# Three passes instead of four for the last 64 queries, keys turned over in place, and the first MoE's relu earlier in the order

## The chip, the core and the metric

The kernel runs on one core of a Trainium2 chip. The core has a matrix engine (TensorE; PE in the profile, with its weight loads shown apart as PEld), a vector engine (VectorE, DVE), a scalar engine (ScalarE, ACT), a general one (GpSimd, POOL) and a queue engine (SyncE, SP) that issues nearly all DMAs here. Each engine works through its own list of instructions in a fixed order, and semaphores hold an instruction until what it needs is there. The metric is the device time of one launch in microseconds (us). Before the change it is 1017.72 us, the median of three runs that lie between 1014.41 and 1018.50.

## What is computed

Three steps follow each other, all in float32 (the weights of the two MoEs come as float64):

```
# attention: 4 batches, 8 heads, 576 positions, 64 wide
scores = (q @ k.T) / 8 + cum[query] - cum[key]      # cum: running sum of log f
scores = where(key > query, -1e9, scores)
attn   = softmax(scores) ; x = attn @ v             # -> 2304 tokens x 512
# first MoE: 512 -> 2048 -> 512
h = x @ w_in ; g = max(0.01 * h, h) ; y = g @ w_out
# second MoE: 512 -> 1536 -> 512
out = ((y @ w_a) * (y @ w_b)) @ w_o
```

## The kernel before

**Parts of a number.** A float32 value is kept as a rounded part (type F32R, called high) and a rest (low); a product needs three matmuls: high by high, high by low, low by high. The first MoE's inputs are the pairs `xh`, `xl`; its relu gives `gh` and `gl`.

**Attention.** A batch is worked off as two blocks `(b, r)`: r=0 has queries 0 to 255, r=1 queries 256 to 575 (320 queries against all 576 keys). Within a block the heads come in pairs; `hp` is the pair, `j` is 0 or 1 for its first or second head. In names such as `s4_2_1_3_0` the numbers are batch, block, head and piece. Batch 0 uses plain float32; batches 1 to 3 do as follows (`att_scores`, L322 to L450):

- A head's queries are loaded twice, one copy in each half of the 128 partitions, and turned over 32 by 32 on DVE into `tq` (L326). `qhh` is their high part (ACT, L337), `qll` the rest (DVE, L338).
- The keys of both heads of a pair are loaded into `xk`, one head in each half of the partitions, and turned over by DVE into another tile, `tk` (L350). There are two `xk` buffers, taken in turn by the pairs, and one `tk`.
- For each head, `ks` (three buffers) has the keys' high part in one half of the partitions (ACT, L356) and their low part in the other (DVE, L357). One matmul of `qhh` with `ks` so gives high queries by both parts of the keys, and a second one with `qll` the low queries by both parts.
- Queries 256 to 511 go 128 at a time through `score`, two passes a tile. The last 64 queries of the two heads of a pair share one tile `s4` of 128 rows, worked off with the second head (j=1): `qhh` and `qll` of either head have 64 blank columns beside their last 64 queries, so that head h-1 adds to the first 64 rows alone and head h to the other 64. The 576 keys are cut in two pieces of 288 columns. That is four passes of 128 by 288 a piece (L432 to L440): `qhh` and `qll` of head h-1 with its `ks`, and `qhh` and `qll` of head h with its own.

DVE then adds scores and decay and takes the row's extreme (L402, L444); ACT does the exponential (L373) and the normalisation (L411, L540); PE turns the probabilities over (`pp`) and multiplies by the values (`av`), two heads at once; ACT and DVE bring the result into `xh` and `xl`.

**First MoE.** Tokens go in 9 groups of 256, the inner width in 8 units per group: `work(i, pr)` calls `l1` (24 matmuls of 256 columns into `h`, then the relu) and, one unit late, `l2` (12 matmuls of 512 columns into `y`). `h` has one buffer. The relu is two instructions on ACT, `gh` (rounded) and `hs` (plain), L881 and L882, and one on DVE, `gl`, L884.

**Order.** Apart from the first block, whose order is a table written out by hand, a scheduler lays the instructions of each engine in a row before the run. It goes by the order in which the program issues them; `tc.high_priority(offset=n)` lets an instruction count as issued n instructions earlier. Block (b, r) is issued in the middle of a group's units, so attention's instructions fill in among the MoE's on all engines. SP's loads are in that order as well, and a load that waits for its buffer holds up all loads behind it. The second MoE follows after all attention; its layers use seven products in place of eight on quarters of the matrices.

Of the kernel before, what the change touches and what calls it, by code (L numbers as in the profile page):

```python
# [8 lines left out]
F32 = mybir.dt.float32  # L9
F32R = mybir.dt.float32r  # L10
# [4 lines left out]
ALU = mybir.AluOpType  # L15
# [3 lines left out]
P = 128  # L19
# [7 lines left out]
def kernel(  # L27
# [14 lines left out]
    B, H, S, D = q.shape  # L42
# [9 lines left out]
    SCALE = 1.0 / float(D) ** 0.5  # L52
# [67 lines left out]
    pe_att, act_att, dve_att, pool_att = (Ahead(e) for e in (nc.tensor, nc.scalar, nc.vector, nc.gpsimd))  # L120
# [12 lines left out]
    def f32(ap):  # L133
        return ap.bitcast(F32)
# [128 lines left out]
    def att_scores(b, r, h, st):  # L263
# [3 lines left out]
        hp, j = h // 2, h % 2  # L267
# [46 lines left out]
        else:  # L314
# [15 lines left out]
            lasts[h] = qhh, qll  # L330
            z0 = 64 if r == 1 and j == 1 else 0
            if r == 1:
                blank = slice(320, 384) if j == 0 else slice(0, 64)
                for part in (qhh, qll):
                    pool_att.memset(f32(part[:, blank]), 0.0)
            zq = slice(z0, z0 + nq)
            act_att.mul(qhh[:, zq], tq[:, :nq], -SCALE)  # L337
            dve_att.scalar_tensor_tensor(  # L338
                out=qll[:, zq], in0=tq[:, :nq], scalar=-SCALE, in1=f32(qhh[:, zq]), op0=ALU.mult, op1=ALU.subtract
            )  # L340
            if j == 0:
                xk = ap_.tile([P, 18, 32], F32, tag=("xk", "xk2")[hp % 2], name=f"xk_{nm}")
                for u in range(2):
                    for e in range(2):
                        nc.sync.dma_start(
                            xk[u * 64 + e * 32 : u * 64 + e * 32 + 32, :nkc, :],
                            k[b, h + u, 0:nk, e * 32 : e * 32 + 32].rearrange("(c i) d -> i c d", i=32),
                        )
                tk = ap_.tile([P, S], F32, tag="tk", name=f"tk_{nm}")
                dve_att.transpose(out=tk[:, :nk], in_=xk[:, :nkc, :].rearrange("p c d -> p (c d)"))  # L350
                qks[pair] = tk

            ks = lastk[h] = ap_.tile([P, S], F32R, tag="ks", bufs=3, name=f"ks_{nm}")
            o = 64 - a
# [2 lines left out]
            dve_att.tensor_tensor(  # L357
                out=ks[o : o + 64, :nk], in0=tk[a : a + 64, :nk], in1=f32(ks[a : a + 64, :nk]), op=ALU.subtract
            )

            def score(o, c0, cols_):
                pe_att.matmul(o, qhh[:, c0 : c0 + P], ks[:, cols_], start=True, stop=False)
# [50 lines left out]
        if r == 1:  # L413
            if j == 0:
                p4s[b, hp] = ap_.tile([P, S], F32, tag="p4", name=f"p4_{nm}")
            p4 = p4s[b, hp]
            st4 = ap_.tile([P, 1], F32, tag="st4", bufs=2, name=f"st4_{nm}")
            made = pool_att.tensor_scalar(
                p4[a : a + 64, :], cumb[a : a + 64, :], 1.0, ncum_t4[a : a + 64, b * HP + hp : b * HP + hp + 1],
                op0=ALU.mult, op1=ALU.add,  # L420
            )
            if (b, h) == (0, 0):
                tc.add_manual_dep(made.ins, quiet[0].ins.name, SYNC, reason="second block's decay behind the fourth pair")
            pool_att.affine_select(
                out=p4[a : a + 64, 512:S], in_=p4[a : a + 64, 512:S], pattern=[[-1, 64]], base=0,
                channel_multiplier=1, compare_op=ALU.is_ge, fill=MASKED,
            )
            for c in range(2):
                if b and j == 0:
                    break  # L430
                sl = slice(c * 288, c * 288 + 288)
                sp = score_bank(b, pair, j, (4, c), f"s4_{nm}_{c}")  # L432
                w = slice(0, P) if b else slice(a, a + 64)
                if b:
                    m = 0
                    for g in (h - 1, h):
                        for part in lasts[g]:
                            two = part[:, 2 * P : 3 * P] if g < h else part[:, 0:P]
                            pe_att.matmul(sp[:, :288], two, lastk[g][:, sl], start=(m == 0), stop=(m == 3))
                            m += 1  # L440
                elif j == 0:
                    scores_of_both(both_heads[pair, (4, c)], (256, 192), sl)
                acc = st4 if c == 0 else stat[:, 0, 4:5]
                dve_att.tensor_tensor_reduce(  # L444
                    out=p4[w, sl], in0=sp[w, :288], in1=p4[w, sl],
                    op0=ALU.add, op1=ALU.min, scale=1.0,
                    scalar=ABOVE if c == 0 else st4[w, :], accum_out=acc[w, :],
                )
                yield
            if j == 1:  # L450
                exp(p4, 4)
                st["rec4"] = over(4, 1)
                yield
# [400 lines left out]
    def l1(i, pr):  # L854
# [22 lines left out]
        gl = mp.tile([P, 2, T1], F32R, tag="gl", name=f"gl_{i}_{pr}")  # L877
        if (i, pr) == (0, 0):
            nc.gpsimd.memset(mp.tile([P, 72], F32, tag="gap1", bufs=1, name="gap1"), 0.0)
        with tc.high_priority(offset=1):  # L880
            nc.scalar.activation(gh, hps, AF.Prelu, alpha=0.01)  # L881
            nc.scalar.activation(hs, hps, AF.Prelu, alpha=0.01)  # L882
        with tc.high_priority(offset=400 if last else 0):
            nc.vector.tensor_tensor(out=gl, in0=hs, in1=f32(gh), op=ALU.subtract)  # L884
        return gh, gl

# [632 lines left out]
```

## Time and profile before

| | |
|---|---|
| median of three runs | 1017.72 us |
| the profiled execution's own time | 1017.11 us |
| its span, first to last instruction | 1015.3 us |
| PE busy | 997.5 us (98%) |
| PE weight loads | 866.4 us (85%) |
| DVE, ACT, POOL busy | 681.1, 547.7, 177.4 us |
| PE in the first 40 us | 30.4 us |

The first 40 us hold the first attention block and the first weights; attention and the first MoE run together until about 490 us; then the rest of the first MoE and the second MoE. Busy PE means that some matmul was in flight: matmuls overlap, so the duration of one (about 0.3 us) is longer than the time from its start to the next one's. The granted clock of PE is 9 tenths or more in every slice. Durations in what follows come from the profiled execution.

### The profile page before, as it was taken

The numbers are of one execution on the slowest core, as the hardware profiler recorded it, in microseconds if no ns is written. First come the engines' busy times: TensorE is split into PE (matmuls) and PEld (weight loads), VectorE is DVE, ScalarE is ACT, GpSimd is POOL, SyncE is SP. The second block draws the span as 40 slices with busy tenths as digits, with TensorE's granted clock in tenths as the row PEclk, the third lists the DMA queues.
The fourth block names the chain that finished last, engine by engine and source line by source line (L and its number), as shares of the span: only waits on it lengthen the run. The fifth ranks groups of instructions, "written<-read, shape, count | busy, mean of one in ns | idle before, by whom it ended". The sixth has DMA issues, their size and how long they took to land.

```text
span 1015.3 us, 18187 instructions
## 1 busy us (share of the span) xinstructions
PE 997.5 (98%) x6435; PEld 866.4 (85%) x6435; DVE 681.1 (67%) x1400; ACT 547.7 (54%) x1125; POOL 177.4 (17%) x404
## 2 busy tenths in 40 slices
PE   7899999999999999999999999999999999999998
PEld 6676778888888888888899998888888888999998
DVE  5889866765554555545277547778686776998982
ACT  7678787977666776667445424332322221444430
POOL 3515425442333323332000000000000000000000
PEclk9999999999999999999999999999999999999999
DMA  8897245545442344422384224232251434847721
GB/s 218 241 277 228 67 74 116 120 86 98 96 80 67 75 89 97 80 55 40 147 294 151 84 57 110 83 131 87 94 166 42 135 119 135 243 133 201 218 74 42
DMA packets 263468, 125.68 MB, mean 124 GB/s; under 512 B 182417, under 2 KB 245265, under 8 KB 263377
## 3 DMA queue, kind: packets, MB, share of 16 engines
q1 hardware_dynamic: 262656, 123.39, 45.5%
q8 instruction: 51, 0.84, 0.3%
q10 hardware_dynamic: 720, 1.12, 0.3%
q14 instruction: 41, 0.33, 0.1%
HBM read 95.29 MB, written 29.17 MB: 123 GB/s over the span
## 4 chain that ended last, share of the span: by engine, by line
PE 83%; DVE 1%; DMA 1%; SPq 1%; ACT 1%; issue 1%; POOL 0%; DVEq 0%; POOLq 0%; ACTq 0%
PE h L865 17%; PE y L899 17%; PE o L1243 12%; PE b_b L1120 5%; PE b_a L1120 5%; PE s L99 4%; PE av L99 4%; PE a_b L1120 3%; PE a_a L1120 3%; PE d_b L1120 3%; PE d_a L1120 3%; PE pp L99 3%; PE a_last L1152 2%; PE b_last L1152 2%; DMA p<-p_dram 1%
## 5 line engine op out<-in xcount | busy, mean ns | idle before, releaser
L865 PE MATMUL h<-xh,homer 128*128 128x256 f32 x1152 | 222.6, 282 | 0.0
L865 PEld LDWEIGHTS h<-xh,homer 128*128 128x128 f32 x1152 | 182.8, 188 | 6.0 <-issue 1.8
L899 PE MATMUL y<-homer,gh 128*128 128x512 f32 x576 | 179.6, 399 | 1.6 <-ACT gh L881 1.4
L865 PE MATMUL h<-xl,homer 128*128 128x256 f32 x576 | 162.1, 281 | 0.0
L899 PEld LDWEIGHTS y<-homer,gh 128*128 128x128 f32 x576 | 103.7, 188 | 22.6 <-ACT gh L881 2.7
L865 PEld LDWEIGHTS h<-xl,homer 128*128 128x128 f32 x576 | 108.4, 188 | 2.8
L899 PE MATMUL y<-homer,gl 128*128 128x512 f32 x288 | 108.7, 396 | 0.0
L390 POOL TENSOR_SCALAR p<-cumb,ncum_t 128x384 f32<-128x384 f32 (+2 forms) x112 | 74.9, 675 | 161.9 <-PE pp L99 78.8
L884 DVE TENSOR_TENSOR gl<-hs,gh 128x512 fp32r<-128x512 f32 x72 | 51.0, 709 | 58.8 <-ACT hs L882 58.3
L373 ACT ACTIVATE p<-p,stat 128x256 f32<-128x256 f32 (+3 forms) x123 | 73.5, 599 | 23.6 <-DVE stat L402 17.0
L1243 PE MATMUL o<-homer,homer 128*128 128x256 f32 x672 | 84.6, 280 | 0.0
L1243 PEld LDWEIGHTS o<-homer,homer 128*128 128x128 f32 x672 | 81.5, 188 | 0.2
L402 DVE CUSTOM_DVE_ANT_0 p<-s,p 128x384 f32<-128x384 f32 (+2 forms) x100 | 48.3, 489 | 44.5 <-PE s L99 35.4
L411 ACT ACTIVATE p<-p,rec 128x384 f32<-128x384 f32 (+1 forms) x108 | 56.1, 568 | 13.8 <-DVE rec L379 13.5
L881 ACT ACTIVATE gh<-h 128x512 fp32r<-128x512 f32 x72 | 42.8, 594 | 36.8 <-PE h L865 35.1
L899 PEld LDWEIGHTS y<-homer,gl 128*128 128x128 f32 x288 | 51.9, 188 | 10.4 <-issue 1.8
L99 PE MATMUL pp<-ident,p 128*128 128x128 f32 (+1 forms) x376 | 58.5, 275 | 0.0
L957 ACT CAST homer<-p 128x1536 fp32r<-128x1536 f32 (+1 forms) x28 | 36.3, 1316 | 27.9 <-DVE p L983 15.4
L99 PEld LDWEIGHTS pp<-ident,p 128*128 128x128 f32 (+1 forms) x376 | 43.4, 139 | 6.5 <-issue 1.6
L958 DVE TENSOR_TENSOR homer<-p,homer 128x1536 fp32r<-128x1536 f32 (+1 forms) x28 | 43.2, 1553 | 6.1 <-ACT homer L957 6.0
L99 PE MATMUL s<-ks,qhh 128*128 128x288 f32 (+4 forms) x144 | 45.8, 327 | 1.0 <-DVE stat L402 0.5
L882 ACT ACTIVATE hs<-h 128x512 f32<-128x512 f32 x72 | 42.8, 594 | 6.6 <-DMA y_dram<-yo 6.6
(274 smaller groups left out, 2005.7 us busy)
## 6 DMA issues: line engine op xcount, KB each, us to landing
p<-p_dram SPq DMA_DIRECT2D x17, 768.0 KB, 5.5
p_dram<-p SPq DMA_DIRECT2D x12, 1024.0 KB, 4.5
cumb<-cum_dram SPq DMA_DIRECT2D x32, 288.0 KB, 3.8
homef<-in_moe_w_out_dram SPq DMA_DIRECT2D x15, 511.6 KB, 6.3
homef<-in_moe_w_in_dram SPq DMA_DIRECT2D x15, 510.5 KB, 5.1
raw_o<-in_moe_w_out_dram SPq DMA_DIRECT2D x12, 511.6 KB, 5.4
xq<-in_q_dram SPq DMA_DIRECT2D x144, 32.0 KB, 2.0
y_dram<-yo SPq DMA_DIRECT2D x72, 64.0 KB, 2.0
```

Of the source, the lines that this page charges most:

```text
L99: return method(*args, **kw)
L373: act_att.activation(pt, pt, AF.Exp, bias=stat[:, 0, s : s + 1], scale=-1.0, accum_out=stat[:, 1, s : s + 1])
L390: made = pool_att.tensor_scalar(pt, cumb[:, :n], 1.0, ncum_t[:, t, bh : bh + 1], op0=ALU.mult, op1=ALU.add)
L402: dve_att.tensor_tensor_reduce(out=pt, in0=sp[:, :n], in1=pt, op0=ALU.add, op1=ALU.min, scale=1.0, scalar=ABOVE, accum_out=stat[:, 0, s : ...
L411: act_att.mul(ps[i], ps[i], rec[:, i : i + 1])
L865: made = nc.tensor.matmul(hps[:, u, :], w[:, c * P : c * P + P], x[:, c, :], start=(n == 0), stop=(n == 3 * ND - 1))
L881: nc.scalar.activation(gh, hps, AF.Prelu, alpha=0.01)
L884: nc.vector.tensor_tensor(out=gl, in0=hs, in1=f32(gh), op=ALU.subtract)
L899: nc.tensor.matmul(ybank[i][z], g[:, u, z * P : z * P + P], w, start=(fi == 0 and n == 0), stop=(fi == NF1 - 1 and n == 2),)
L958: next_in("dve", nc.vector.tensor_tensor(out=lo, in0=src, in1=f32(hi), op=ALU.subtract))
L1120: nc.tensor.matmul(to, w[:, W_ROWS[m], wl, c2 * P : c2 * P + P], y[c2][xl_][:, Y_COLS[m], :], start=(first and c2 == e == 0), stop=(c2 == ...
L1243: nc.tensor.matmul(ps[m], xps[n, j // 3][:, X_ROWS[m], xl_, j % 3, :], wo2[j][:, O_COLS[m], wl, :], start=(j == e == y == 0), stop=(j == N ...
```

## The change

Three edits, two of them in `att_scores` for batches 1 to 3.

**Three passes.** For the last 64 queries, the two passes with `qll` become one. The low part of the last 64 queries of both heads is written into one tile, that of head h-1, as two blocks: its own in partitions 0 to 63, columns 256 to 319, and that of head h in partitions 64 to 127, columns 320 to 383; the other two quarters are blank. The weights of that pass are these 128 columns, and it runs against a new tile, `lastk[hp, "both"]` (named `kh`): the rounded keys of both heads, one ACT copy of 128 by 576 for each pair. (The product of low queries with low keys of these rows is no longer taken.) On DVE, `qll` is now written as one piece of 128 by 256 and, for r=1, one of 64 by 64. On POOL, each pair still has four memsets for the blanks, two of them now of 64 by 64. `kh` takes the buffer with the tag `tk`.

**Keys turned over in place.** For r=1, DVE's transpose writes back into `xk`; `ks` and `kh` are then made from `xk`, whose buffer is so held until the second head's copies are done. For r=0 the transpose still goes to `tk`.

**Relu.** In `l1` the two ACT instructions have an offset of 150 in place of 1, and DVE's `gl` one of 150 in place of 0 (the last two groups keep 400 for `gl`).

```
-            blank = slice(320, 384) if j == 0 else slice(0, 64)
-                for part in (qhh, qll):
-                    pool_att.memset(f32(part[:, blank]), 0.0)
-            zq = slice(z0, z0 + nq)
-            act_att.mul(qhh[:, zq], tq[:, :nq], -SCALE)
-            dve_att.scalar_tensor_tensor(out=qll[:, zq], in0=tq[:, :nq], ...)
+                pool_att.memset(f32(qhh[:, slice(320, 384) if j == 0 else slice(0, 64)]), 0.0)
+                if j == 0:
+                    pool_att.memset(f32(qll[0:64, 320:384]), 0.0)
+                    pool_att.memset(f32(qll[64:P, 256:320]), 0.0)
+            act_att.mul(qhh[:, z0 : z0 + nq], tq[:, :nq], -SCALE)
+            rests = [(qll, slice(0, P), lead + z0, lead, 2 * P)]
+            if r == 1:
+                rests.append((lasts[h - j][1], slice(a, a + 64), 256 + a, 0 if j else 256, 64))
+            for to, rows_, at, from_, n in rests:
+                dve_att.scalar_tensor_tensor(out=to[rows_, at : at + n], ...)
...
-                tk = ap_.tile([P, S], F32, tag="tk", name=f"tk_{nm}")
-                dve_att.transpose(out=tk[:, :nk], in_=xk[:, :nkc, :].rearrange("p c d -> p (c d)"))
-                qks[pair] = tk
+                tk = xk[:, :nkc, :].rearrange("p c d -> p (c d)")
+                turned_k = tk if r else ap_.tile([P, S], F32, tag="tk", name=f"tk_{nm}")[:, :nk]
+                dve_att.transpose(out=turned_k, in_=tk)
+                tk = qks[pair] = turned_k
...
+            if r == 1 and j == 1:
+                lastk[hp, "both"] = ap_.tile([P, S], F32R, tag="tk", name=f"kh_{nm}")
+                act_att.copy(lastk[hp, "both"], tk)
...
-                    for g in (h - 1, h):
-                        for part in lasts[g]:
-                            two = part[:, 2 * P : 3 * P] if g < h else part[:, 0:P]
-                            pe_att.matmul(sp[:, :288], two, lastk[g][:, sl], start=(m == 0), stop=(m == 3))
+                    for m, (two, keys) in enumerate(
+                        ((lasts[h - 1][0][:, 2 * P : 3 * P], lastk[h - 1]),
+                         (lasts[h][0][:, 0:P], lastk[h]),
+                         (lasts[h - 1][1][:, 2 * P : 3 * P], lastk[hp, "both"]))):
+                        pe_att.matmul(sp[:, :288], two, keys[:, sl], start=(m == 0), stop=(m == 2))
...
-        with tc.high_priority(offset=1):
+        with tc.high_priority(offset=150):
             nc.scalar.activation(gh, hps, AF.Prelu, alpha=0.01)
             nc.scalar.activation(hs, hps, AF.Prelu, alpha=0.01)
-        with tc.high_priority(offset=400 if last else 0):
+        with tc.high_priority(offset=400 if last else 150):
             nc.vector.tensor_tensor(out=gl, in0=hs, in1=f32(gh), op=ALU.subtract)
```

What it does to the order is seen at three places. The first is PE at the last queries of heads 2 and 3 in batch 2, block 1; `s4_2_1_3_0` is the first piece of 288 keys, `h` and `y` are the first MoE's products. Before:

```order
L99 MATMUL s4_2_1_3_0_4776<-ks_2_1_2_4631,qhh_2_1_2_4618 128x288
L99 MATMUL s4_2_1_3_0_4776<-ks_2_1_2_4631,qll_2_1_2_4619 128x288
L99 MATMUL s4_2_1_3_0_4776<-ks_2_1_3_4723,qhh_2_1_3_4717 128x288
L99 MATMUL s4_2_1_3_0_4776<-ks_2_1_3_4723,qll_2_1_3_4718 128x288
L899 MATMUL y_3_0_4140<-homer_16384_2048_930,gh_3_4_4266 128x512 x2
```

The same piece and the next one with the change:

```order
L99 MATMUL s4_2_1_3_0_4784<-ks_2_1_2_4637,qhh_2_1_2_4623 128x288
L877 MATMUL h_3_5_4287<-xh_3_2034,homer_22528_2048_1159 128x256
L99 MATMUL s4_2_1_3_0_4784<-ks_2_1_3_4729,qhh_2_1_3_4723 128x288
L99 MATMUL s4_2_1_3_0_4784<-kh_2_1_3_4732,qll_2_1_2_4624 128x288
L99 MATMUL s4_2_1_3_1_4789<-ks_2_1_2_4637,qhh_2_1_2_4623 128x288
L99 MATMUL s4_2_1_3_1_4789<-ks_2_1_3_4729,qhh_2_1_3_4723 128x288
L99 MATMUL s4_2_1_3_1_4789<-kh_2_1_3_4732,qll_2_1_2_4624 128x288
```

A piece has three matmuls of 288 columns where it had four, and the third needs `kh`. The second place is ACT at the same pair of heads. Before, with `p4` the probabilities of the last queries of the pair before it:

```order
L337 ACTIVATE qhh_2_1_2_4618<-tq_2_1_2_4616 128x320
L356 CAST ks_2_1_3_4723<-tk_2_1_2_4629 64x576
L500 COPY pt_2_1_0_4546<-pp_2_1_1_0_4645 128x3x128
L373 ACTIVATE p4_2_1_0_4518,stat_2_1_0_4467<-p4_2_1_0_4518,stat_2_1_0_4467 128x576
L337 ACTIVATE qhh_2_1_3_4717<-tq_2_1_3_4715 128x320
L356 CAST ks_2_1_4_4813<-tk_2_1_4_4811 64x576
```

And with the change:

```order
L337 ACTIVATE qhh_2_1_2_4623<-tq_2_1_2_4621 128x320
L362 CAST ks_2_1_3_4729<-xk_2_1_2_4631 64x576
L362 CAST ks_2_1_4_4820<-xk_2_1_4_4814 64x576
L369 CAST kh_2_1_3_4732<-xk_2_1_2_4631 128x576
L512 COPY pt_2_1_0_4553<-pp_2_1_1_0_4651 128x3x128
L383 ACTIVATE p4_2_1_0_4523,stat_2_1_0_4471<-p4_2_1_0_4523,stat_2_1_0_4471 128x576
L512 COPY pt_2_1_0_4553<-pp_2_1_1_1_4657 128x4x128
L337 ACTIVATE qhh_2_1_3_4723<-tq_2_1_3_4721 128x320
```

The copy `kh` stands 15 rows ahead of the relu of unit 4 of that group, and the next pair's first `ks` has moved ahead of it. The third place is ACT at the relu of unit 3 of group 1, while heads 5 and 6 of batch 1, block 0 are normalised (`p_1_0_6_0`, `rec` is what DVE gives for it). Before:

```order
L337 ACTIVATE qhh_1_1_0_2575<-tq_1_1_0_2573 128x320
L356 CAST ks_1_1_1_2641<-tk_1_1_0_2586 64x576
L411 ACTIVATE p_1_0_5_0_2179<-p_1_0_5_0_2179,rec_1_0_5_2_2205 128x128
L411 ACTIVATE p_1_0_5_1_2195<-p_1_0_5_1_2195,rec_1_0_5_2_2205 128x256
L456 CAST xh_3_2034<-av_1_0_2_2144 128x64
L373 ACTIVATE p_1_0_6_0_2234,stat_1_0_6_2210<-p_1_0_6_0_2234,stat_1_0_6_2210 128x128
L373 ACTIVATE p_1_0_6_1_2250,stat_1_0_6_2210<-p_1_0_6_1_2250,stat_1_0_6_2210 128x256
L411 ACTIVATE p_1_0_6_0_2234<-p_1_0_6_0_2234,rec_1_0_6_0_2269 128x128
L881 ACTIVATE gh_1_3_1845<-h_1_3_1819 128x512
L882 ACTIVATE hs_1_3_1844<-h_1_3_1819 128x512
```

And with the change:

```order
L421 ACTIVATE p_1_0_5_0_2179<-p_1_0_5_0_2179,rec_1_0_5_2_2205 128x128
L421 ACTIVATE p_1_0_5_1_2195<-p_1_0_5_1_2195,rec_1_0_5_2_2205 128x256
L893 ACTIVATE gh_1_3_1845<-h_1_3_1819 128x512
L894 ACTIVATE hs_1_3_1844<-h_1_3_1819 128x512
L468 CAST xh_3_2034<-av_1_0_2_2144 128x64
L337 ACTIVATE qhh_1_1_0_2575<-tq_1_1_0_2573 128x320
L362 CAST ks_1_1_1_2642<-xk_1_1_0_2583 64x576
```

The relu no longer stands behind the exponentials and the first normalisation of head 6, but ahead of `qhh_1_1_0`.

## Rows read from the trace of the kernel before

**Rows 1.** The page: busy time of each engine; PE's granted clock in 40 slices, tenths.
```profile
PE 997.5 (98%) x6435; PEld 866.4 (85%) x6435; DVE 681.1 (67%) x1400; ACT 547.7 (54%) x1125; POOL 177.4 (17%) x404
...
PEclk9999999999999999999999999999999999999999
```

**Rows 2.** Windows: stretch and its us, busy us (and instructions) by engine, PEclk, DMA.
```profile
core 0: us, PE busy (x) PEld busy (x) DVE busy (x) ACT busy (x) POOL busy (x), PEclk, DMA share, GB/s
...
40.00:180.00 140.00, 135.62 (x857) 103.56 (x854) 111.54 (x265) 111.08 (x261) 58.88 (x106) 1.00 0.62 159
180.00:490.00 310.00, 310.00 (x2152) 271.38 (x2151) 170.23 (x518) 223.85 (x559) 106.64 (x261) 1.00 0.40 79
490.00:1015.00 525.00, 521.54 (x3230) 468.05 (x3228) 373.93 (x537) 184.75 (x241) 0.00 (x0) 1.00 0.43 133
```

**Rows 3.** PE's waits, 90 to 180 us: releaser, us in total, times, longest.
```profile
PE y L899 <- ACT gh L881: 0.8, 1, 0.8
PE s L99 <- DVE stat L402: 0.5, 1, 0.5
PE s L99 <- DVE stat L113: 0.4, 1, 0.4
PE s L99 <- DVE st L113: 0.3, 1, 0.3
PE y L899 <- ACT hs L882: 0.2, 1, 0.2
```

**Rows 4.** Groups by form, 130 to 490 us: PE's passes of 288 columns.
```profile
L99 PE MATMUL s<-ks,qhh 128*128 128x288 f32 x48 | 13.7, 300 | 0.0
L99 PE MATMUL s<-ks,qll 128*128 128x288 f32 x48 | 13.4, 297 | 0.0
```

**Rows 5.** Timeline of PE at one pair's eight passes: start, duration, instruction.
```profile
193.60 0.29 PE L99 MATMUL s<-ks,qhh 128*128 128x288 f32 x1
...
194.53 0.29 PE L99 MATMUL s<-ks,qll 128*128 128x288 f32 x1
194.75 2.28 PE L99 MATMUL av<-pt,vn 128*64 128x320 f32 x20
...
211.88 1.03 PE L99 MATMUL av<-pt,vn 128*64 128x320 f32 x6
```

**Rows 6.** Timeline of PE, ACT and DVE at one relu.
```profile
166.27 0.18 DVE L457 TENSOR_TENSOR xl<-av,xh 128x64 fp32r<-128x64 f32 x1
...
166.82 0.40 ACT L411 ACTIVATE p<-p,rec 128x128 f32<-128x128 f32 x1 [1.17 <-DVE rec L379]
167.13 0.58 ACT L881 ACTIVATE gh<-h 128x512 fp32r<-128x512 f32 x1
...
167.76 0.50 PE L899 MATMUL y<-homer,gh 128*128 128x512 f32 x1 [0.80 <-ACT gh L881]
```

**Rows 7.** Groups by form, 130 to 490 us: what the added instructions resemble.
```profile
L356 ACT CAST ks<-tk 64x576 fp32r<-64x576 f32 x24 | 16.1, 672 | 2.0 <-DVE tk L350 0.9 <-DVE rec L378 0.5
L338 DVE SCALAR_TENSOR_TENSOR qll<-tq,qhh 128x320 fp32r<-128x320 f32 x24 | 12.8, 534 | 3.1 <-ACT qhh L337 2.9
L338 DVE SCALAR_TENSOR_TENSOR qll<-tq,qhh 128x256 fp32r<-128x256 f32 x23 | 10.1, 440 | 4.0 <-ACT qhh L337 3.6
L540 ACT ACTIVATE p<-p,rec 128x576 f32<-128x576 f32 x12 | 9.3, 775 | 1.3 <-DVE rec L379 1.3
L350 DVE STREAM_TRANSPOSE tk<-xk 128x576 f32<-128x576 f32 x12 | 9.1, 757 | 3.4 <-DMA xk<-in_k_dram 3.4
```

**Rows 8.** One line's answer, the load of the keys (L345): landing times.
```profile
DMA to landing us min/median/max: 1.6/2.4/4.8
```

**Rows 9.** Groups by form, 130 to 490 us: the relu's first instruction.
```profile
L881 ACT ACTIVATE gh<-h 128x512 fp32r<-128x512 f32 x43 | 25.5, 594 | 11.8 <-PE h L865 11.6
```

**Rows 10.** Windows: the block of batch 1 with 320 queries.
```profile
180.00:240.00 60.00, 60.00 (x428) 52.85 (x427) 40.43 (x125) 52.15 (x127) 24.54 (x61) 1.00 0.51 97
```

More of the change, by code (lines that the diff above doesn't have):

```diff
@@ L332, in att_scores @@
             if r == 1:
-                blank = slice(320, 384) if j == 0 else slice(0, 64)
-                for part in (qhh, qll):
-                    pool_att.memset(f32(part[:, blank]), 0.0)
-            zq = slice(z0, z0 + nq)
-            act_att.mul(qhh[:, zq], tq[:, :nq], -SCALE)
-            dve_att.scalar_tensor_tensor(
-                out=qll[:, zq], in0=tq[:, :nq], scalar=-SCALE, in1=f32(qhh[:, zq]), op0=ALU.mult, op1=ALU.subtract
-            )
+                pool_att.memset(f32(qhh[:, slice(320, 384) if j == 0 else slice(0, 64)]), 0.0)
[7 more added lines that the diff above has]
+            for to, rows_, at, from_, n in rests:
+                dve_att.scalar_tensor_tensor(
+                    out=to[rows_, at : at + n], in0=tq[rows_, from_ : from_ + n], scalar=-SCALE,
+                    in1=f32(qhh[rows_, z0 + from_ : z0 + from_ + n]), op0=ALU.mult, op1=ALU.subtract,
+                )
             if j == 0:
@@ L434, in att_scores @@
                 if b:
-                    m = 0
-                    for g in (h - 1, h):
-                        for part in lasts[g]:
-                            two = part[:, 2 * P : 3 * P] if g < h else part[:, 0:P]
-                            pe_att.matmul(sp[:, :288], two, lastk[g][:, sl], start=(m == 0), stop=(m == 3))
-                            m += 1
+                    for m, (two, keys) in enumerate(
+                        (
+                            (lasts[h - 1][0][:, 2 * P : 3 * P], lastk[h - 1]),
+                            (lasts[h][0][:, 0:P], lastk[h]),
+                            (lasts[h - 1][1][:, 2 * P : 3 * P], lastk[hp, "both"]),
+                        )
+                    ):
+                        pe_att.matmul(sp[:, :288], two, keys[:, sl], start=(m == 0), stop=(m == 2))
                 elif j == 0:
```

## The prediction

> **What bounds the kernel now.** I read the page first, then the windows, then PE's waits, and last the rows of single instructions. The page has PE busy for 997.5 of 1015.3 us, at full clock after the second slice [rows 1]; every other engine is at 67% or less. That average hides where the slack is, so the windows come next [rows 2]. The change touches attention of batches 1 to 3 and the relu, that is 40 to 490 us. From 180 to 490 us, where nearly all of the changed passes lie, PE is busy 310.00 of 310 us, while ACT has 223.85 and DVE 170.23: here the time is the sum of PE's work, and a matmul taken out shortens it. From 40 to 180 us PE is idle for 140 - 135.62 = 4.4 us, so an earlier instruction on ACT or DVE can give something back there, and only there. After 490 us PE is the bound again, and the change does not reach it. The waits between 90 and 180 us, where the order starts to differ, come to 0.8 + 0.5 + 0.4 + 0.3 + 0.2 = 2.2 us, and the first of them is the relu's: `y` waits for `gh` [rows 3].
>
> **The passes.** There are 3 batches, 4 pairs and 2 pieces of keys: 24 products of four passes, which are the 48 + 48 rows of 288 columns [rows 4]. One pass in four goes: 24. What one costs is not its duration of 300 or 297 ns, since matmuls overlap, but the time from its start to the next start. At one pair's eight passes the first starts at 193.60 and the eighth at 194.53 [rows 5]: 0.93 / 7 = 0.133 us. So 24 x 0.133 = 3.2 us leave PE, all of it in stretches without idle PE, and I count it in full.
>
> The Trainium skill ("TensorE: Matmul & The Clock Gate", section "Wait — 56ns, not 53.3ns?") puts back-to-back matmuls at full clock at the columns over 2.4 GHz plus about 2.5 ns, which is an estimate of 122.5 ns for 288 columns; by it the term would be 2.9 us. The row is a tenth longer, and the sum goes by the row.
>
> **The copy of the keys.** Each of the 12 pairs gets one ACT copy of 128 by 576. The trace of before has no such copy; the nearest rows are the rounding copy of 64 by 576 at 672 ns and the scaling of 128 by 576 at 775 ns [rows 7]. I take 0.672 (the same operation and columns), 8.1 us of ACT in all, with 9.3 us as the other end. It lies beside PE's work: ACT has 310 - 223.85 = 86 us free between 180 and 490 us [rows 2]. PE needs it for the third pass of a piece, and the scheduler has put it some 15 ACT rows ahead of a relu whose unit PE works off before that pass, so I count nothing on the path. Without that cover it would cost between nothing and all 9.3 us (below: the slower rival).
>
> **DVE and POOL.** The rest of the queries goes from 24 instructions of 320 columns (534 ns) to 24 of 256 (440 ns) and 24 of 64 by 64 [rows 7]. For the small one the nearest row is a subtraction of 128 by 64 at 0.18 us [rows 6]; that makes -2.26 + 4.32 = +2.1 us on an engine with 140 us free. The transposes in place number 12 of 757 ns [rows 7]. The trace has none in place; were one to take twice as long, that would be 9.1 us more on DVE, and were it to take no time, 9.1 us less. I take the row as it is; either end is hidden by the same 140 us. The memsets stay four a pair. All of this I count at nothing, because PE's work covers it.
>
> **What is held longer.** `xk` is now free for the pair after next only when the second head's copies are done, not when the transpose is. The order shows the key loads some rows later on SP, and what stands behind one of them (queries, decay rows, values, stores of `y`) waits with it. A key load lands after 2.4 us, 4.8 at most [rows 8], and the transpose takes 0.76 us. One pair's products with the values start at 194.75 and the next pair's at 211.88 [rows 5], so a pair lasts 17 us and the buffer has most of that to be filled again. I count nothing; if it were not hidden, the third and fourth pair of three blocks would each wait, 6 x 2.4 = 14 us, and PE would fill part of that with the first MoE. In return the single `tk` no longer ties one pair's transpose to the copies of the pair before it, which can win at most the waits that PE has there, and from 180 us on it has none.
>
> **The relu.** The 0.8 us are one place: ACT reaches `gh` at 167.13, 0.40 us and a wait of 1.17 us for DVE behind the normalisation of head 6, and PE's `y` starts at 167.76 after 0.80 us of waiting [rows 6]. In the new order this relu stands ahead of head 6's exponentials and normalisation, so that wait goes: -0.8 us. What is late next at that place is head 6's normalisation, behind two instructions of 0.594 us [rows 9] for each unit, 1.2 us; PE has the unit's matmuls meanwhile. The other waits of `y` in this stretch are 0.2 us. The relu is moved past attention's steps at all units from the second half of group 0 on, and each time these wait up to 1.2 us; from 180 us on this can win nothing, since PE never waits, and it loses nothing as long as PE has units to work on.
>
> **The sum.** 3.2 + 0.8 = 4.0 us off the profiled execution's own 1017.11 us (a span of 1015.3 and 1.8 around it) give 1013.1. The median of the three runs is 0.6 us above that execution, which would make it 1013.7; I say 1013.4.
>
> **Rivals.**
>
> *The remaining waits go too.* The order from 90 us on is another one on every engine, and s and y stand in fewer and longer runs. If all 2.2 us of rows 3 went, the time would be 1017.1 - 3.2 - 2.2 = 1011.7; if all 4.4 us of idle PE between 40 and 180 us went, 1009.5. For it: the waits are on ACT and DVE results whose order the change moves. Against: those of the scores (0.5, 0.4, 0.3) are on a score bank that DVE has yet to read, which no offset changes, and the wait-heavy part ahead of 90 us keeps its order.
>
> *Given back.* The passes are fewer, but PE only seems full: a busy PE counts overlapped matmuls, and its weight loads are busy 271.38 of 310 us, so 39 us could be slack [rows 2]. Then the chain of one pair (scores, DVE, ACT, turning, values) sets the pace, 3.2 us of PE work turn into waits, and the time stays at 1017.1 to 1017.7. Against: starts follow each other at 0.133 us with nothing between [rows 5], and no wait of PE shows after 180 us.
> The Trainium skill ("Perfetto Trace Analysis", section "Identifying the Most-Contended Engine") says that matmul busy time is no good measure and that headroom is to be judged by the weight loads' busy share. By that rule PE has an eighth left in this stretch and this rival would be the likeliest; the starts speak against it, and I leave it a small chance.
>
> *ACT becomes the bound (slower).* In the block of batch 1 with 320 queries ACT is busy 52.15 of 60 us [rows 10], 87%; four copies of up to 0.775 make it 55.3. Its list is worked off in order, and the relus now push attention's steps back. It decides from the point where ACT's work in such a block reaches PE's, 60 us less the block's share of the passes, 59. If every copy came onto the path, the time would be 1017.1 - 3.2 + 9.3 = 1023.2; if only those of batch 1 did, 1017.1 - 3.2 + 3.1 = 1017.0. Against: 4 us stay free even in the fullest block, and the other two blocks are emptier (223.85 of 310 over all).
>
> **How the numbers follow.** The forecast, 1013.4, has 0.56, with a range of its own from 1011.9 to 1015.5 (what reordering may add or take at other places, about 2 us, as much as the waits there now); the waits gone as well, 0.20; given back, 0.13; ACT as the bound, 0.11. The low end is 1009.5, where all idle PE of 40 to 180 us is gone. The high end is 1019: past the time given back, with part of ACT's copies on the path; what lies above is most of the last rival. About 0.5%, 5.1 us, is what a measurement of this kernel can tell from no change, so faster means below 1012.6. That is most of the second case (0.18) and a third of the first (0.18): 0.36. Slower means above 1022.8, which takes nearly all copies on the path or a load that is not hidden: 0.08. The rest, 0.56, is within it.
>
> **What would show it.** In the profile after: 72 passes of 288 columns in place of 96, PE still at 310 of 310 in the same stretch, which now ends some 4 us earlier; no `y` that waits 0.8 us for `gh` near 167 us; 12 copies near 0.7 us and ACT some 8 us busier; `xk` landing before its transpose is due. The forecast is wrong if PE shows waits for `kh`, for ACT's exponentials or for `xk` between 180 and 490 us, if the stretch to 490 us is not shorter by the passes, or if the part after it changes.

## The result: 0.5% slower

The changed kernel takes 1023.10 us, the median of 22 runs, beside 1017.76 us, the median of 22 runs of the kernel before: a ratio of 1.0054 with a 95% interval from 1.0041 to 1.0066. That is 5.3 us more where 4 less were predicted, and above the range. (One of the 22 runs before took 2515.25 us; the ratio is of fast runs and leaves it out.)

The page after has the same picture as [rows 1]: PE 98% busy, at full clock after the start. (In rows of after, line numbers from the first changed line on are up to 12 higher: `gh` is L893, the transposes L356.)

```profile
PE 999.9 (98%) x6411; PEld 863.2 (85%) x6411; DVE 686.0 (67%) x1424; ACT 551.4 (54%) x1137; POOL 176.7 (17%) x404
...
PEclk9899999999999999999999999999999999999999
```

The windows, columns as in [rows 2], show where it went:

```profile
40.00:180.00 140.00, 137.35 (x866) 105.27 (x867) 109.15 (x262) 109.27 (x255) 56.08 (x97) 1.00 0.62 157
180.00:490.00 310.00, 304.59 (x2082) 261.81 (x2080) 177.34 (x540) 225.14 (x569) 105.72 (x267) 1.00 0.41 79
...
490.00:1021.00 531.00, 527.15 (x3271) 472.83 (x3269) 374.45 (x542) 189.75 (x250) 0.00 (x0) 1.00 0.42 131
```

From 40 to 180 us PE idles 2.65 us, where it idled 4.4. From 180 to 490 us it idles 5.4 us, where it had none, and works off 2082 matmuls in this time, not 2152; 25 of the 70 that are missing are passes of 288 columns. The last `y` of the first MoE starts 6.0 us later than before; first the row of before, then that of after:

```profile
616.28 0.39 PE L899 MATMUL y<-homer,gl 128*128 128x512 f32 x1
```
```profile
622.28 0.39 PE L911 MATMUL y<-homer,gl 128*128 128x512 f32 x1
```

So all of the loss lies ahead of the second MoE. The passes took 3.2 us of work away and the stretch is 6.0 us longer: by this sum some 9.2 us are new stalls. The idle time shows only 3.7 of them (5.4 us more from 180 to 490 us, 1.7 us less from 40 to 180). The rest hides in the way busy time counts: the profile shows a matmul of `h` in flight for 0.28 us while the next one can start after 0.12, so a stall of 0.16 us leaves no gap. It can be counted by starts instead: how much later each matmul starts than the median for that pair of shapes in the kernel before, from 100 to 520 us, delays over 60 ns, most of them regular in both kernels. Before has 41.5 us by this count and after 50.0: 8.5 more.

PE's waits from 180 to 490 us; before has none in this stretch:

```profile
PE pp L99 <- ACT p L421: 2.1, 3, 0.8
PE y L911 <- ACT gh L893: 1.7, 2, 1.1
PE s L99 <- DVE stat L412: 0.8, 2, 0.7
PE av L99 <- ACT pt L509: 0.4, 1, 0.4
```

The groups by form, 130 to 500 us, have the answer to [rows 4] and [rows 7] in their first four rows, and in the last one what was not expected. Its last columns are the idle time just ahead of the instruction and what ended it:

```profile
L99 PE MATMUL s<-ks,qhh 128*128 128x288 f32 x48 | 10.5, 300 | 0.0
L99 PE MATMUL s<-kh,qll 128*128 128x288 f32 x24 | 7.1, 295 | 0.0
L369 ACT CAST kh<-xk 128x576 fp32r<-128x576 f32 x12 | 8.1, 672 | 0.1
L342 DVE SCALAR_TENSOR_TENSOR qll<-tq,qhh 64x64 fp32r<-64x64 f32 x24 | 6.0, 249 | 0.3
L356 DVE STREAM_TRANSPOSE xk<-xk 128x576 f32<-128x576 f32 x12 | 9.3, 778 | 36.8 <-DMA xk<-in_k_dram 36.8
```

There are 72 passes, the copies take 0.672 us as costed, and DVE stands 36.8 us in front of the 12 transposes, waiting for keys; before it stood 3.4 us [rows 7]. What such a stop does is seen near the end of block (2, 0). DVE:

```profile
253.72 0.08 DVE L412 DVE_READ_ACCUMULATOR2_ANT stat<- 128x1 f32 x1
256.88 0.78 DVE L356 STREAM_TRANSPOSE xk<-xk 128x576 f32<-128x576 f32 x1 [3.09 <-DMA xk<-in_k_dram]
257.59 0.13 DVE L388 TENSOR_SCALAR rec<-stat 128x2 f32<-128x2 f32 x1
257.75 0.17 DVE L389 RECIPROCAL rec<-rec 128x2 f32<-128x2 f32 x1
...
260.30 0.78 DVE L356 STREAM_TRANSPOSE xk<-xk 128x576 f32<-128x576 f32 x1 [1.99 <-DMA xk<-in_k_dram]
```

ACT's normalisations, which need `rec`, with one exponential between them, and PE, which turns the result over:

```profile
258.01 0.80 ACT L421 ACTIVATE p<-p,rec 128x128 f32<-128x128 f32 x2 [2.30 <-DVE rec L389]
...
261.44 0.51 ACT L383 ACTIVATE p<-p,stat 128x256 f32<-128x256 f32 x1 [0.67 <-DVE stat L412]
...
263.48 0.80 ACT L421 ACTIVATE p<-p,rec 128x128 f32<-128x128 f32 x2 [1.01 <-DVE rec L389]
```
```profile
262.97 0.28 PE L877 MATMUL h<-xl,homer 128*128 128x256 f32 x1
263.08 0.28 PE L877 MATMUL h<-xh,homer 128*128 128x256 f32 x1
263.93 0.33 PE L99 MATMUL pp<-ident,p 128*128 128x128 f32 x1 [0.57 <-ACT p L421]
```

DVE idles 3.09 us, `rec` behind it is late, and ACT waits 2.30 us for it. The second stop, 1.99 us, makes a row extreme late: ACT's exponential waits 0.67 us for it, the next `rec` comes 1.01 us late for the normalisation behind, and PE then needs 0.85 us from start to start (263.08 to 263.93), where the starts before were 0.11 apart. Not every stop is paid for: the longest two, 6.17 us at 318.7 and 6.28 at 416.9, fall where DVE has nothing urgent, and PE's starts beside them run on. Of the 8.5 us by starts, 5.9 lie at 180 to 200, 250 to 280 and 380 to 400 us; in the last two stretches a block with 256 queries, whose heads are short, gives way to one with 320 (batches 2 and 3).

### The profile page after: what moved, and what is told of

Its sections match the earlier page's. It is cut to its first block, busy times and chain, and to the rows that moved or that the text cites. A ratio compares the mean times of both kernels' runs of the same rounds, so it can differ in the third digit from the quotient of the medians.

```text
span 1021.2 us, 18206 instructions
## 1 busy us (share of the span) xinstructions
PE 999.9 (98%) x6411; PEld 863.2 (85%) x6411; DVE 686.0 (67%) x1424; ACT 551.4 (54%) x1137; POOL 176.7 (17%) x404
## 4 chain that ended last, share of the span: by engine, by line
PE 77%; DMA 8%; ACT 4%; DVE 4%; SPq 3%; issue 2%; POOL 1%; ACTq 0%; POOLq 0%; DVEq 0%
PE y L911 14%; PE h L877 14%; PE o L1255 12%; PE b_b L1132 5%; PE b_a L1132 5%; PE s L99 4%; PE a_b L1132 3%; PE a_a L1132 3%; PE d_b L1132 3%; PE d_a L1132 3%; PE av L99 3%; PE pp L99 3%; DMA o_dram<-c_o 2%; PE a_last L1164 2%; PE b_last L1164 2%
## 5 line engine op out<-in xcount | busy, mean ns | idle before, releaser
L877 PE MATMUL h<-xh,homer 128*128 128x256 f32 x1152 | 225.4, 283 | 0.4 <-ACT hs L894 0.3
L911 PE MATMUL y<-homer,gh 128*128 128x512 f32 x576 | 177.5, 399 | 2.4 <-ACT gh L893 2.3
L400 POOL TENSOR_SCALAR p<-cumb,ncum_t 128x384 f32<-128x384 f32 (+2 forms) x112 | 71.3, 643 | 145.4 <-PE pp L99 73.0
L893 ACT ACTIVATE gh<-h 128x512 fp32r<-128x512 f32 x72 | 42.5, 590 | 32.5 <-PE h L877 31.1
L412 DVE CUSTOM_DVE_ANT_0 p<-s,p 128x384 f32<-128x384 f32 (+2 forms) x100 | 47.1, 487 | 13.9 <-PE s L99 6.7
L99 PE MATMUL av<-pt,vn 128*64 128x320 f32 (+4 forms) x400 | 44.7, 363 | 0.5 <-ACT pt L509 0.4
L403 POOL TENSOR_SCALAR_AFFINE_SELECT p<-p 128x128 f32<-128x128 f32 x112 | 44.1, 410 | 2.3
```

The source lines that it names most:

```text
L99: return method(*args, **kw)
L400: made = pool_att.tensor_scalar(pt, cumb[:, :n], 1.0, ncum_t[:, t, bh : bh + 1], op0=ALU.mult, op1=ALU.add)
L403: pool_att.affine_select(out=pt[:, t * P : n], in_=pt[:, t * P : n], pattern=[[-1, P]], base=0, channel_multiplier=1, compare_op=ALU.is_ge ...
L412: dve_att.tensor_tensor_reduce(out=pt, in0=sp[:, :n], in1=pt, op0=ALU.add, op1=ALU.min, scale=1.0, scalar=ABOVE, accum_out=stat[:, 0, s : ...
L877: made = nc.tensor.matmul(hps[:, u, :], w[:, c * P : c * P + P], x[:, c, :], start=(n == 0), stop=(n == 3 * ND - 1))
L911: nc.tensor.matmul(ybank[i][z], g[:, u, z * P : z * P + P], w, start=(fi == 0 and n == 0), stop=(fi == NF1 - 1 and n == 2),)
```

## Experiments

Theory A: turning the keys over in place holds `xk`, the loads come late, DVE stands. Theory B: the relu's priority pushes attention back. Theory C: the copy `kh`. Every run below was timed beside the kernel before in five rounds; ratios are to it. "Stop" is DVE's idle time ahead of the 12 big transposes (140 to 500 us, groups by form).

### Which of the three edits (e1 to e4)

e1 is the kernel before with the transposes in place alone; e2 has the relu's offsets alone; e3 is the changed kernel without them; e4 has both, with four passes.

```
e1, e4 (before)  - tk = ap_.tile(tag="tk"); transpose(out=tk, in_=xk)
                 + turned_k = tk if r else ap_.tile(tag="tk"); transpose(out=turned_k, in_=tk)   # tk = view of xk
e2, e4 (before)  - offset=1 / 0      + offset=150      (gh, hs / gl)
e3 (after)       - offset=150        + offset=1 / 0
```

> The kernel before with one edit: for r=1 the keys are turned over in place in xk; four passes and the old relu order stay. Theory A (in place, xk is held until the second head's ks copies are done, its next load is issued late, and DVE, which works in order, sits before the transpose until the load lands; in the changed kernel that is 36.8 us of DVE waiting where before had 3.4): the loss is here too, ratio 1.004 to 1.009 (some 1022 to 1027 us), with DVE waiting over 20 us for xk. Theory B (the relu's higher priority pushes attention's steps back): no change, 0.998 to 1.002. Theory C (the copy kh is the loss): no change either, 0.998 to 1.002.

> The kernel before with one edit: the relu's three instructions have an offset of 150. Theory A: 0.998 to 1.001, no loss, since xk is freed by the transpose as before. Theory B: the loss is here, 1.004 to 1.010, and PE waits for ACT's p and DVE's stat between 180 and 500 us. Theory C: 0.998 to 1.001.

> The changed kernel with the relu's old offsets (three passes, kh and in place stay). Theory A: the load waits stay, ratio 1.001 to 1.006. Theory B: the passes' 3.2 us come out clean, 0.996 to 0.998. Theory C: 1.003 to 1.006.

> The kernel before with two edits, in place and the relu's offsets, and four passes. Theory A: the changed kernel's loss without the passes' gain, 1.006 to 1.011. Theory B: the same range. Theory C: 0.998 to 1.002.

| run | edits | ratio | 95% interval | stop |
|---|---|---|---|---|
| e1 | in place | 1.0137 | 1.0110 to 1.0164 | 45.2 us |
| e2 | relu | 1.0007 | 0.9990 to 1.0024 | 0.0 us |
| e3 | passes, in place | 1.0056 | 1.0033 to 1.0078 | 38.9 us |
| e4 | in place, relu | 1.0104 | 1.0080 to 1.0129 | 44.3 us |
| after | all three | 1.0054 | 1.0041 to 1.0066 | 36.8 us |

The loss is the transposes in place: 13.9 us by themselves, above the range that I gave. B and C fall: the relu alone changes nothing, and kernels without `kh` lose more, not less. Why in place alone costs more than together with the passes stays open.

### Attempts to shorten the hold (e5, e6, e8, e11)

```
e5 (e3)   - ks of the second head and kh made with j == 1      + both made with j == 0
e6 (e3)   - dve_att.transpose(...)                             + (nc.vector if r else dve_att).transpose(...)   # no lead of 300
e8 (e3)   - xk: two tags; cumb: bufs=3                         + xk: three tags; cumb: bufs=2
e11 (e3)  - xk: two tags                                       + r=1: third tag, cumb's third buffer
```

> Three passes and in place, old relu offsets; for r=1 both heads' ks and kh are made with the first head, right behind the transpose, so that xk is free about one head's time (some 8 us) earlier. Theory A (the loss is the time for which xk is held): DVE's wait for xk falls from 37 us to under 15 and the ratio to 0.996 to 1.001, against 1.0056 with the copies at the second head. Theory A' (what costs is the transpose in place as such, or the other order that comes with it, and not the holding): 1.003 to 1.008, and the waits stay.

> Three passes and in place, old relu offsets; the transposes of r=1 lose their lead of 300 in the order, so that DVE has other work ahead of them while the load is under way. xk is held as long as before. Theory A in its DVE form (the harm is that DVE, working in order, stands before the transpose while rows for ACT and PE are ready): DVE's wait for xk under 15 us and a ratio of 0.997 to 1.002. If the harm is the late keys themselves (scores come late whatever DVE does meanwhile): 1.004 to 1.010.

> Three passes and in place, old relu offsets, with a third buffer for xk (room again from cumb with two buffers): the holding stays, but the next load no longer waits for it. Theory A: DVE's wait for xk under 10 us, ratio 0.996 to 1.000. Theory A' (in place as such): 1.003 to 1.008.

> Three passes and in place, old relu offsets; for r=1 a third xk buffer takes the place of the third decay buffer, batch 0 keeps three. Theory A: the holding no longer delays the loads; DVE waits under 15 us for xk, ratio 0.996 to 1.001. Theory A' (in place as such, whatever the buffers): 1.003 to 1.008.

Ratios: e5 1.0055 (1.0036 to 1.0073), stop 38.2 us; e6 1.0037 (1.0020 to 1.0053), stop 38.4; e8 1.0110 (1.0080 to 1.0139); e11 1.0050 (1.0031 to 1.0069), stop 30.5. All four missed what theory A expected, because none did what it was meant to: the stop stays near 30 us or above (e8: 29.8 us for the 11 transposes in the window). In e5 the second head's copy comes as late as in e3 (27 us behind the first head's at the second pair of batch 2, in both), presumably for want of a `ks` buffer; in e6 the scheduler filled DVE's list much as before; e11's decay rows wait on SP for the buffer that keys now share with them (14.3 us). e8, with two decay buffers all through, takes 0.5% more than e3; its trace has 133.10 of 140 us busy from 40 to 180 us, against 134.77, and why it loses more stays open. e5 and e11 lie where the rival beside A was expected (in place as such, whatever the buffers: 1.003 to 1.008), e6 fits neither. Since the stops stayed, these runs do not decide about A; e15 below, which is in place too, speaks against the rival.

### The other two edits without in place (e7, e9, e10, e12)

`kh` needs room of its own when `tk` stays. e7 takes it from the decay rows all through, e9 and e10 only in r=1 of batches 1 to 3; e12 is the price of that room alone.

```
e7 (e3)    - turned_k = tk if r else ap_.tile(tag="tk")   + turned_k = ap_.tile(tag="tk")
           - kh: tag="tk"; cumb: bufs=3                   + kh: tag="kh"; cumb: bufs=2
e9         as e7, but kh: tag="cumb3"; cumb: tags "cumb", "cumb2" if b and r else all three
e10        as e9, offset=150 for the relu
e12 (before)  cumb: tags "cumb", "cumb2" if b and r else all three
```

> Three passes, old relu offsets, keys turned over into tk as before and kh in a buffer of its own; the room comes from the decay rows (cumb, two buffers in place of three). Theory A: no DVE wait for xk to speak of (under 5 us) and the passes' 3.2 us come out: 0.996 to 0.999, if two decay buffers cost nothing. Theory C (kh or the passes themselves bring the loss): 1.002 to 1.006.

> Three passes, old relu offsets, keys turned over into tk as before. kh takes the third decay buffer, and the decay rows of r=1 in batches 1 to 3 use two; batch 0 keeps three, unlike in the run with two decay buffers all through, whose loss lay in 40 to 180 us (PE busy 128.2 of 140). Theory A (the loss is what in-place transposes do to the key loads): PE busy at least 135 of 140 from 40 to 180 us and 320 of 320 from 180 to 500, DVE waiting under 5 us for xk, ratio 0.995 to 0.999. Theory C (kh and the passes bring the loss): 1.002 to 1.007.

> The same with the relu's offsets of 150. Theory A: the whole change without the transposes in place, 0.994 to 0.999. Theory B (the relu's priority costs once ACT has kh too): 1.002 to 1.007.

> The kernel before with the decay rows of r=1 in batches 1 to 3 on two buffers and nothing else: the price of the room that the two runs beside it take. 0.999 to 1.002 by every theory; if more, that much comes off them.

e7: 1.0065 (1.0041 to 1.0089), a miss in the number, but the windows tell why: its loss is ahead of 180 us, where it has two decay buffers in the first blocks too, and behind that PE is full.

```profile
40.00:180.00 140.00, 128.20 (x770) 97.63 (x770) 102.54 (x236) 101.07 (x228) 52.72 (x90) 0.96 0.57 146
180.00:500.00 320.00, 320.00 (x2212) 279.40 (x2212) 183.66 (x572) 239.34 (x603) 106.87 (x277) 1.00 0.42 83
```

With batch 0 left alone, e9 has 0.9966 (0.9950 to 0.9981), e10 0.9947 (0.9928 to 0.9966), and e12 1.0013 (0.9996 to 1.0030). e9's windows and its transposes:

```profile
40.00:180.00 140.00, 137.53 (x882) 106.26 (x879) 111.98 (x272) 113.52 (x265) 61.92 (x113) 1.00 0.65 161
180.00:490.00 310.00, 310.00 (x2143) 270.68 (x2143) 174.44 (x537) 227.21 (x568) 97.84 (x254) 1.00 0.40 78
```
```profile
L362 DVE STREAM_TRANSPOSE tk<-xk 128x576 f32<-128x576 f32 x12 | 9.0, 749 | 2.3 <-DMA xk<-in_k_dram 2.3
```

PE is full again, DVE stops for 2.3 us, and 0.34% of 1018.4 is 3.5 us: the passes' 3.2 us come out. e10, at a median of 1013.25 us, is faster than both kernels by its ratio. It is the change with `tk` kept and a decay buffer given up for it.

### The hold, or the place in the list (e13, e14)

e13 puts the hold into e9: a tiny addition reads `xk` and the second head's `ks`. e14 keeps e3's hold and moves its key loads on SP.

```
e13 (e9)  + dve_att.tensor_tensor(out=seen, in0=held[hp][:, 0, 0:1], in1=f32(ks[:, 0:1]), op=ALU.add)     # j == 1, r == 1; held[hp] is the pair's xk
e14 (e3)  + with tc.high_priority(offset=200 if r else 0):   # around the four loads of xk
```

> The version with three passes, kh in a buffer of its own and keys turned over into tk (0.9966 of the time before), with one thing added: 12 DVE additions of 128 by 1 that read xk and the second head's ks, so that xk is held until those copies are done, as in the changed kernel, although nothing is turned over in place. (Their results go nowhere.) If the holding is the loss: DVE waits over 20 us for xk again and the ratio goes back to 1.002 to 1.008. If the transpose in place as such is the loss: 0.995 to 0.999, DVE waiting under 5 us for xk.

> Three passes, in place, old relu offsets; the four loads of a pair's keys for r=1 get an offset of 200, so that they stand together on SP ahead of the next heads' query loads, where the changed kernel has up to 12 query loads of 0.47 us between them. xk is held as long as before. If the place in SP's list is what makes the keys late: DVE's wait for xk falls under 20 us, ratio 0.996 to 1.002. If the holding by itself is enough: DVE's wait stays over 25 us (SP then stands at the first piece, and the queries come late too), 1.003 to 1.009.

e13: 0.9983 (0.9968 to 0.9999), stop 2.0 us. e14: 1.0057 (1.0037 to 1.0076), stop 16.0 us. So the hold alone does not bring the loss, which is against theory A. It does make e13's key loads late: SP issues those of the third and fourth pair of block (2, 1) from 278 and 304 us on (before 261 and 279, after 282 and 306); but there they still land 16.4 and 8.8 us before their transposes start. e14 fits neither of its two expectations: it halves DVE's stops, and the loss stays. By place that is less odd. In batches 2 and 3, e3 stops for 8.9 us at the first two pairs of a block and for 23.7 us at the last two; e14 has 12.0 and 1.5. It took away stops in the long blocks, where those of 6.2 and 6.3 us above cost nothing, and left those at 250 to 260 and 376 to 390 us. (From 40 to 180 us e14's PE is also busy 1.4 us less than e3's.) What the changed kernel, e3 and e14 share, and e13 lacks, is how early the transposes stand. The transposes in DVE's list around the first two pairs of block (2, 1), in the changed kernel, with row numbers:

```
483 STREAM_TRANSPOSE tk_2_0_6            <- keys of r=0, heads 6 and 7
490 STREAM_TRANSPOSE xk_2_1_0            <- keys of r=1, heads 0 and 1
496 STREAM_TRANSPOSE xk_2_1_2            <- keys of r=1, heads 2 and 3
503 STREAM_TRANSPOSE tq_2_0_6            <- queries of r=0, head 6
511 STREAM_TRANSPOSE tq_2_0_7
```

In the kernel before the two of r=1 stand in rows 504 and 526, the second 22 rows behind the first. There is one `tk`, so a transpose cannot stand ahead of the copies that read the pair before it. Without `tk` nothing keeps it back: theory D.

### Theory D: only the order (e15 to e18)

```
e15 (e3)     + if r and hp: tc.add_manual_dep(transpose, low keys of head h-1, ORDER)    # place in the list, no semaphore
e16 (after)  + the same
e18 (e3)     + the same, and for hp == 0 behind the low keys of r=0, head 7
e17 (e12)    - tk: tag="tk"    + tk: tag="cumb3" if r and hp % 2 else "tk"     # a second tk
```

> Three passes, in place, old relu offsets, as in e3 (1.0056), with one thing added: an order (no semaphore) that keeps a pair's transpose in DVE's list behind the second head's low keys of the pair before, where the single tk had kept it. xk is held exactly as long. Theory D (it is the place of the transpose in DVE's list: without tk nothing keeps it back, so it stands early and DVE stops there until the load lands): DVE's wait for xk under 15 us, 0.995 to 1.001. Theory A (the holding delays the load, wherever the transpose stands): 1.003 to 1.009, the waits stay over 25 us.

> The whole changed kernel (1.0054) with the same order added. Theory D: 0.993 to 1.000. Theory A: 1.003 to 1.008.

> The kernel before on two decay buffers for r=1 (1.0013 by itself) with the third as a second tk: xk is free at the transpose, so nothing is held, and nothing keeps a transpose behind the pair before. Theory D: transposes stand early again (the second pair's of batch 2 12 to 14 rows behind the first's, where before had 22), DVE waits over 15 us for xk and the ratio is 1.003 to 1.010. Theory A (the holding is needed for the loss): 0.999 to 1.003.

> e15 (0.9996) with the same order for the first pair of r=1 too: its transpose stands behind the low keys of the last head of r=0. e15 still has DVE waits of 3.3 and 2.1 us there. If these waits are what is left between e15 and the version that is not in place (0.9966): DVE's wait for xk under 4 us and a ratio of 0.995 to 0.998. If what is left is the holding of xk (two key buffers for r=1 in place of three): 0.998 to 1.002.

| run | ratio | 95% interval | against |
|---|---|---|---|
| e15 | 0.9996 | 0.9977 to 1.0016 | e3 1.0056 |
| e16 | 0.9974 | 0.9958 to 0.9990 | after 1.0054 |
| e18 | 0.9994 | 0.9980 to 1.0008 | e15 0.9996 |
| e17 | 1.0035 | 1.0020 to 1.0051 | e12 1.0013 |

The transposes of e15, of e18, of e17 and of e16:

```profile
L358 DVE STREAM_TRANSPOSE xk<-xk 128x576 f32<-128x576 f32 x12 | 9.3, 779 | 7.3 <-DMA xk<-in_k_dram 7.0
```
```profile
L358 DVE STREAM_TRANSPOSE xk<-xk 128x576 f32<-128x576 f32 x12 | 9.3, 778 | 2.1 <-DMA xk<-in_k_dram 1.7
```
```profile
L356 DVE STREAM_TRANSPOSE tk<-xk 128x576 f32<-128x576 f32 x12 | 9.3, 771 | 8.6 <-DMA xk<-in_k_dram 5.9 <-POOL p L396 1.5 <-issue 1.2
```
```profile
L358 DVE STREAM_TRANSPOSE xk<-xk 128x576 f32<-128x576 f32 x12 | 9.3, 779 | 6.8 <-DMA xk<-in_k_dram 3.9 <-DMA vn<-in_v_dram 2.7
```

One order relation, with the hold and the buffers as they were, takes 0.6% off e3 and 0.8% off the changed kernel; the intervals are apart. That is shown. Where the time went is seen from the changed kernel to e16, whose stop falls from 36.8 to 6.8 us and whose PE idles 0.3 us from 180 to 490 us in place of 5.4:

```profile
180.00:490.00 310.00, 309.74 (x2134) 269.62 (x2134) 176.40 (x548) 230.64 (x578) 99.83 (x267) 1.00 0.41 80
```

(e3 and e15 cannot be compared so: their profiled executions, 1018.72 and 1018.57 us, lie 4.0 us below and 2.9 us above their medians.) But the order is not all of it. e17 has transposes that stand early with nothing held: its stop of 8.6 us is under the 15 that I expected, and its interval touches e12's. e13 has the hold with late transposes: 0.17% above e9, the intervals overlapping. e3 has both and is 0.90% above e9. So it seems to take both, transposes that stand early and loads that the hold delays; how much either does alone is too small for these runs. e18 takes the last stops away and gains nothing, so what is left between it and e9 (0.28%, the intervals just touch) is not DVE's stop. It may be the hold, which e13 has too (0.9983, between the two), or that in place `kh` shares `tk`'s buffer with the keys of r=0; no run tells these two apart.

## Why the prediction was wrong, step by step

**What bounds the kernel.** Right: PE is the bound, and where nothing stalls it a pass taken out is time taken out. The rival "given back" would have left e9 at the time of before; it has 0.9966. The Trainium skill's rule for judging PE's headroom by the weight loads' busy share ("Perfetto Trace Analysis", section "Identifying the Most-Contended Engine") does not fit this stretch: by it an eighth was free, and e9 gained the passes in full at 270.68 of 310 us. What I set aside, though that rival says it, is that 310 of 310 does not mean "no stall up to now, none possible": the count cannot see stalls under 0.16 us.

**The passes.** Right in mechanism and size: 3.2 us predicted; e9 gives 3.5, the price of its room included, with an interval from 1.9 to 5.1.

**The copies, DVE, POOL.** Right: 8.1 us of ACT in copies of 0.672, hidden; no engine waits for `kh`. The 64 by 64 rests take 0.249 us, not 0.18, which adds 1.7 us to DVE, hidden too; the transpose in place takes 0.778 us against 0.757. "ACT becomes the bound" named the right time (1023.2) for the wrong reason: ACT's idle time did not shrink to nothing (225.14 busy of 310), and e9 has the same copies.

**What is held longer: the step that failed.** I looked at the hold as a question of whether a load fits into 17 us, and counted nothing, with 14 us as the bad end. Beside it I wrote that `tk` "no longer ties one pair's transpose to the copies of the pair before it", and put that down as a possible gain. Its going is most of the loss: with the tie put back as an order and nothing else, the ratio falls from 1.0056 to 0.9996 (e15) and from 1.0054 to 0.9974 (e16). That tie was what kept each transpose in DVE's list until its keys had landed: in nine of the 12 pairs of the kernel before, they lay there for 8 to 37 us. Without it the scheduler set the transpose ahead of work that was ready, 3 to 19 us before the copies that read it, and each of the 12 started at most 0.2 us after its last piece had landed. Nor had the buffer most of 17 us: in after the second head's low keys end 12.0 to 45.3 us behind the pair's transpose, so the loads go out late. A piece then landed 2.7 us after issue in the median, 5.1 at most, hardly later than in [rows 8]; but its four pieces were also spread out on SP, where one waits for the buffer and 12 query loads stand ahead of the next three:

```profile
297.58 0.44 SPq L377 DMA_DIRECT2D cumb<-cum_dram  x1
306.42 0.31 SPq L350 DMA_DIRECT2D xk<-in_k_dram  x1
306.93 0.35 SPq L322 DMA_DIRECT2D xq<-in_q_dram  x1
...
312.73 0.40 SPq L377 DMA_DIRECT2D cumb<-cum_dram  x1
313.18 1.51 SPq L350 DMA_DIRECT2D xk<-in_k_dram  x3
```

SP stands for 8.4 us, then issues queries for 5.8. The prediction followed PE's, ACT's and SP's lists, and not DVE's, where the two transposes of rows 490 and 496 stand ahead of queries of the block before. Nor could the sign that I had named show it: PE never waits for `xk`; DVE does, for 36.8 us where the sum had nothing.

**The relu.** The wait of 0.8 us at that place is gone: from 90 to 180 us PE waits for `gh` 0.6 us in after, and for some of what else stood in [rows 3]:

```profile
PE y L911 <- ACT gh L893: 0.6, 2, 0.4
PE s L99 <- DVE stat L412: 0.5, 1, 0.5
PE s L99 <- DVE stat L113: 0.2, 1, 0.2
```

But e2, the relu alone, has 1.0007: waits for `gh` of 2.3 us came at other places from 90 to 490 us, so the term was given back. Its -0.8 us is smaller than the interval of any run here. With the passes and `tk` kept, e10 is 0.2% faster than e9, and the intervals overlap.

**The sum.** -4.0 us was predicted for three edits; e10, which is two of them and the price of the room, has -5.4 us (interval -7.3 to -3.5). The third edit, counted at nothing, brought the sign.

## What to carry to other kernels

A buffer that ties two steps together is also what orders them in a scheduler's list: before it is removed, look where the freed instruction will stand, and what stands behind it on an engine that works in order. If it waits for a DMA there, a plain order relation may give back most of what the buffer did: here 0.6 of the 0.9% between e3 and e9. And a stretch in which PE is busy all the time can still lose time, since overlapping matmuls cover short stalls; compare starts, or the matmuls done by a given time.

## What the runs showed that was not expected

- DVE's stops are cheap or dear by place: 6.2 us at 318.7 us cost PE nothing at that place, 3.1 and 2.0 us at 256.9 and 260.3 held it up 0.7 us a step later; in e14 the stops fell from 38.9 to 16.0 us with no gain, since those that went were mostly of the first kind.
- Three edits did not add up: in place costs 1.4% with four passes and, against e9, 0.9% with three.
- Two decay buffers in place of three all through: e7's PE is busy 128.20 of the 140 us from 40 to 180 us, against 137.53 in e9, which has three for batch 0; in e8, with two as well, it is 133.10 against e3's 134.77. Where only r=1 of batches 1 to 3 has two, the price is 0.1%, not clear of the noise (0.9996 to 1.0030).
